# Moving the loads of v, one token-order turn and the start's memsets in a fused attention and MLP kernel

## The chip, the cores and the metric

The kernel runs on one core of a Trainium2 chip. The metric is the device time of one execution in microseconds (us), the median of several runs. A profiled execution gives the trace; its span (317.2 us for the kernel before) is a little shorter than the timed figure.

The core's engines run their own instruction streams in order and meet at semaphores: PE (TensorE, matmuls), DVE (VectorE), ACT (ScalarE), POOL (GpSimd) and SP (SyncE, which here only issues transfers). POOL issues transfers too.

## The reference: what is computed

Attention over 8 batch rows with 8 heads, 576 tokens and 64 channels a head, and then an MLP with a squared relu over all 4608 tokens:

```python
scores = scale * np.matmul(q, k.transpose(0, 1, 3, 2))
rel = pos[:, None] - pos[None, :]
mask_plain = (rel >= 0) & (rel < 32)                        # heads 0 to 3: sliding
mask_dil = (rel >= 0) & (rel < 128) & (rel % 4 == 0)        # heads 4 to 7: dilated
attn = softmax(where(mask, scores, -1e9))
x = (attn @ v).transpose(0, 2, 1, 3).reshape(4608, 512)
g = np.maximum(x @ w_in, 0) ** 2                            # w_in: 512 x 2048
out = g @ w_out                                             # w_out: 2048 x 512
```

"Row" below is a batch row (0 to 7), "block" is a group of 512 tokens of the MLP (0 to 8). The MLP of block b - 1 is computed while the attention of row b is.

## The kernel before

q and k of rows 0 and 1 are transposed on the PE. For row 2 onward they go another way. POOL loads q and k of the sliding heads into `ns` and copies those of the dilated heads to DRAM as fp16 (`dd`). A copy engine writes `ns` in token order into `nr`. SP stores `nr` to DRAM (`dp`) and then reads `dp` and `dd` back with transposing transfers into `QKTp` and `QKTd`:

```python
    def by_token(b, n):
        r = natp.tile([P, 9, HH, D], FP16, name=f"nr{b}", tag="n")
        (nc.gpsimd if b == 2 else nc.vector).tensor_copy(
            r.rearrange("x j h d -> x h j d"), n.rearrange("x h (j d) -> x h j d", d=D)
        )
        return r
    # keep_sliding_qk: two nc.sync.dma_start, dp <- nr
    # transpose_sliding: two nc.sync.dma_start_transpose, QKTp <- dp
    # transpose_dilated: two nc.sync.dma_start_transpose, QKTd <- dd
```

v is loaded by SP in fp32 into the single buffers `sv` (sliding heads) and `sd` (dilated heads), and POOL casts them to fp16 into `vp` and `vd`, of which there are two each:

```python
    def load_v(b):
        load_sliding_v(b)              # two transfers into sv
        load_dilated_v(b, nc.sync)     # two transfers into sd

    def cast_v(b):
        cast_sliding_v(b)              # three POOL copies, vp[b % 2] <- sv
        cast_dilated_v(b)              # four POOL copies, vd[b % 2] <- sd
```

Before POOL loads q and k of a further row it reads one element of the last transpose of the current one:

```python
    def after_transposes(b):
        t = QKTp[b % 2][...] if b == 2 else QKTd[b % 2][...]
        nc.gpsimd.tensor_copy(seen, t)
```

The main loop over the rows. `pump(n)` puts n pieces of the pending MLP work into the instruction streams; `hooks` are called inside the attention of the row: 2 and 3 behind the two groups of dilated scores, 4 to 6 behind the three sliding products with v:

```python
    for b in range(2, B):
        pending.append(moe_gen(b - 1))
        nxt = b + 1
        hooks = {}
        if nxt < B:
            after_transposes(b)
            ns = load_sliding_qk(nxt)
            if b == 2:
                cast_v(b)
            dd = keep_dilated_qk(nxt)
            if b > 2:
                load_v(nxt)
                cast_v(nxt)

            def turn():
                dp = keep_sliding_qk(nxt, by_token(nxt, ns))
                transpose_sliding(nxt, dp)
                transpose_dilated(nxt, dd)
                if b == 2:
                    load_v(nxt)
                    cast_v(nxt)

            hooks[{3: 6}.get(b, 3)] = turn
        first, gap, gap2 = {2: (24, 4, 2), 3: (16, 3, 3)}.get(b, (8, 3, 3))
        pump(first)
        attn_scores(b, gap, 0, hooks)
        attn_values(b, gap2, False, hooks)
        pump(1000)
```

The start: q and k of row 0 are loaded, the masks of the two head groups are built on DVE from an iota on POOL, buffers are cleared, and only then does DVE come to the first copy behind the PE's transposes:

```python
    nsd = {0: load_qk(0)}
    nc.vector.memset(sv[0:PADP, :, 0, :], 0.0)
    nc.vector.memset(sd[0:64, 0, :, :], 0.0)
    nc.gpsimd.iota(reli, ...)
    # ... warm-up of the ScalarE table
    nc.vector.tensor_copy(relf, reli)
    # ... nine DVE instructions: lo_, hi_, maskp / maskd
    nc.vector.memset(sv[0:PADP, :, 1:NB, :], 0.0)
    nc.vector.memset(AT[:, :, UW:640], 0.0)
    for r in range(2):
        # ... five small memsets of QKTp, QKTd, vp, vp, vd, and one compare into vd
    # ...
    nc.vector.tensor_copy(sv[64:P, 0, :, 0], n[0:64, 0, 0:NB])
    load_sliding_v(0)
    nc.vector.tensor_copy(sd[64:P, :, 0, 0], n[0:64, 0, 0:2])
    load_dilated_v(0, nc.sync)
    cast_sliding_v(0, (0, 2))
    load_w_in()
```

The row's MLP work, as far as it matters here: `ph` (PE) is x times w_in, `rt` (ACT) its relu, `g` (DVE) the square; `gs` are sums of `g` on DVE for a Strassen form of the second product, whose results `pa`, `pb`, `pc` are taken by ACT and DVE into `ou` and `ov` and stored.

Of the kernel before, what the change touches and what calls it, by code (L numbers as in the profile page):

```python
# [9 lines left out]
FP32 = mybir.dt.float32  # L10
I16 = mybir.dt.int16
ALU = mybir.AluOpType
ACTF = mybir.ActivationFunctionType
P = 128
# [3 lines left out]
def kernel(  # L18
# [9 lines left out]
    nc = tc.nc  # L28

    B, H, S, D = q.shape  # L30
# [16 lines left out]
    NB = S // QB  # L47
    PADP = P - QB
# [4 lines left out]
    KPAD = 64  # L53
    UW = 576

    const = ctx.enter_context(tc.tile_pool(name="const", bufs=1))
# [29 lines left out]
    QKTp = [const.tile([P, 2, 2, PADP + S], FP16, name=f"QKTp{r}") for r in range(2)]  # L86
    QKTd = [const.tile([P, 2, 2, KPAD + S], FP16, name=f"QKTd{r}") for r in range(2)]
    AT = const.tile([P, 8, 640], FP16, name="AT")
    vp = [const.tile([P, NB, HH, D + 2], FP16, name=f"vp{r}") for r in range(2)]
    vd = [const.tile([P, 2, DIL, HH, D + 2], FP16, name=f"vd{r}") for r in range(2)]  # L90
    sv = stg.tile([P, HH, NB, D], FP32, name="sv")
# [6 lines left out]
    def load_qk(b):  # L98
        n = load_sliding_qk(b)
        m = natp.tile([P, 36 * D], FP16, name=f"nd{b}", tag="n")  # L100
        for i, s in ((1, k), (0, q)):
            nc.gpsimd.dma_start(
                out=m[64 * i : 64 * (i + 1), :],
                in_=s[b, HH:H].rearrange("h (p j) d -> (h p) (j d)", j=36),
            )
        return n, m

    def load_sliding_qk(b):
        n = natp.tile([P, HH, 9 * D], FP16, name=f"ns{b}", tag="n")
        for i, s in ((1, k), (0, q)):  # L110
            nc.gpsimd.dma_start(
                out=n[64 * i : 64 * (i + 1)],
                in_=s[b, 0:HH].rearrange("h (p j) d -> p h (j d)", j=9),
            )
        return n
# [8 lines that stand above are left out]
    def load_sliding_v(b):  # L124
        vv = v[b, 0:HH].rearrange("h (m p) d -> p h m d", p=QB)
        if b == 0:
            for m in range(NB):
                nc.sync.dma_start(out=sv[PADP:P, :, m, :], in_=vv[:, :, m, :])
        else:
            for h in (0, 2):  # L130
                nc.sync.dma_start(out=sv[PADP:P, h : h + 2], in_=vv[:, h : h + 2])

    def load_dilated_v(b, eng):
        vv = v[b, HH:H].rearrange("h (i c) d -> i h (c d)", c=DIL)
        i0 = 0
        for t in range(2):
            eng.dma_start(out=sd[P - OWND[t] : P, t, :, :], in_=vv[i0 : i0 + OWND[t]])
            i0 += OWND[t]

    def load_v(b):  # L140
        load_sliding_v(b)
        load_dilated_v(b, nc.sync)
# [25 lines left out]
    def cast_sliding_v(b, ms=range(0, NB, 2)):  # L168
        for m in ms:
            nc.gpsimd.tensor_copy(  # L170
                vp[b % 2][:, m : m + 2, :, 0:D], sv[:, :, m : m + 2, :].rearrange("p h m d -> p m h d")
            )

    def cast_dilated_v(b):
        for t in range(2):
            p0 = 64 * t
            for c in range(0, DIL, 2):
                nc.gpsimd.tensor_copy(  # L178
                    vd[b % 2][p0:P, t, c : c + 2, :, 0:D],
                    sd[p0:P, t, :, D * c : D * (c + 2)].rearrange("p h (c d) -> p c h d", d=D),  # L180
                )
# [12 lines left out]
    def cast_v(b):  # L194
        cast_sliding_v(b)
        cast_dilated_v(b)


    def keep_dilated_qk(b):
        d = dpool.tile([2, HH * CL, DIL * D], FP16, name=f"dd{b}", tag="dd")  # L200
        for i, src in ((1, k), (0, q)):
            nc.gpsimd.dma_start(
                out=d[i].rearrange("(r i) x -> r (i x)", i=4),
                in_=src[b, HH:H].rearrange("h (r i) d -> (h r) (i d)", i=16),
                max_dma_last_dim=4096,
            )
        return d

    def keep_sliding_qk(b, r):
        d = dpool.tile([2, S, HH * D], FP16, name=f"dp{b}", tag="dp")  # L210
        for i in (1, 0):
            nc.sync.dma_start(
                out=d[i].rearrange("(p j) x -> p (j x)", j=9),
                in_=r[64 * i : 64 * (i + 1)].rearrange("p j h d -> p (j h d)"),
            )
        return d

    def transpose_sliding(b, dp):
        for i in (1, 0):
            nc.sync.dma_start_transpose(out=QKTp[b % 2][:, i, :, PADP:], in_=dp[i])  # L220

    def transpose_dilated(b, dd):
        for i in (1, 0):
            nc.sync.dma_start_transpose(out=QKTd[b % 2][:, i, :, KPAD:], in_=dd[i])
# [4 lines left out]
    def after_transposes(b):  # L229
        t = QKTp[b % 2][:, 0, 1, PADP : PADP + 1] if b == 2 else QKTd[b % 2][:, 0, 1, KPAD : KPAD + 1]  # L230
        nc.gpsimd.tensor_copy(seen, t)


    nsd = {0: load_qk(0)}
    nc.vector.memset(sv[0:PADP, :, 0, :], 0.0)
    nc.vector.memset(sd[0:64, 0, :, :], 0.0)
    reli = const.tile([P, QB], I16, name="reli")
    nc.gpsimd.iota(reli, pattern=[[1, QB]], base=0, channel_multiplier=-1)
    make_identity(nc, ident)
    warm = const.tile([P, 1], FP32, name="warm")  # L240
    nc.vector.memset(warm, 0.0)
    nc.scalar.activation(warm, warm, ACTF.Exp)

    relf = const.tile([P, QB], FP32, name="relf")
    nc.vector.tensor_copy(relf, reli)
# [3 lines left out]
    for m, w, pad in (  # L249
# [12 lines left out]
            lo_[:, 0:w].unsqueeze(1).to_broadcast([P, m.shape[1], w]),  # L262
            hi_[:, 0:w].unsqueeze(1).to_broadcast([P, m.shape[1], w]),
        )
    nc.vector.memset(sv[0:PADP, :, 1:NB, :], 0.0)
    nc.vector.memset(AT[:, :, UW:640], 0.0)
    for r in range(2):
        nc.vector.memset(QKTp[r][:, 1, :, 0:PADP], 0.0)
        nc.vector.memset(QKTd[r][:, 1, :, 0:KPAD], 0.0)
        nc.vector.memset(vp[r][:, :, :, D : D + 1], 1.0)  # L270
        nc.vector.memset(vp[r][0:PADP, 0, :, D : D + 1], 0.0)
        nc.vector.memset(vd[r][:, 1, :, :, D : D + 1], 1.0)
        nc.vector.tensor_scalar(
            out=vd[r][:, 0, :, :, D],
            in0=relf[:, 0:1].unsqueeze(2).to_broadcast([P, DIL, HH]),
            scalar1=-PADD[0] + 0.5,
            scalar2=None,
            op0=ALU.is_lt,
        )
# [3 lines left out]
    for t, w in zip(wi, wi_cols):  # L283
        r = t.rearrange("p d (g f s) -> p d g f s", f=P, s=4)
# [196 lines left out]
    def moe_gen(c):  # L481
        g = hidden(c)
        yield from mm1_gen(c, g, c > 1)
        yield from (mm2_strassen_gen if c > 1 else mm2_gen)(c, g)
# [10 lines left out]
    def pump(n):  # L495
        for _ in range(n):
            while pending:
                try:
                    next(pending[0])
                    break  # L500
                except StopIteration:
                    pending.pop(0)
# [159 lines left out]
    def attn_scores(b, gap, less=0, hooks={}):  # L662
        for hp in range(2):
            s_sliding(b, hp)
            if hp in hooks:
                hooks[hp]()
            pump(gap)
        for g in range(2):
            s_dilated(b, g)
            if 2 + g in hooks:  # L670
                hooks[2 + g]()
            if g:
                halo_sliding(b, 0)
            pump(gap - less)
# [110 lines left out]
# [7 lines that stand above are left out]
            if b == 2:  # L792
                cast_v(b)
            dd = keep_dilated_qk(nxt)
            if b > 2:
                load_v(nxt)
                cast_v(nxt)

            def turn():
                dp = keep_sliding_qk(nxt, by_token(nxt, ns))  # L800
                transpose_sliding(nxt, dp)
                transpose_dilated(nxt, dd)
                if b == 2:
                    load_v(nxt)
                    cast_v(nxt)

            hooks[{3: 6}.get(b, 3)] = turn
        first, gap, gap2 = {2: (24, 4, 2), 3: (16, 3, 3)}.get(b, (8, 3, 3))
        pump(first)
        attn_scores(b, gap, 0, hooks)  # L810
        attn_values(b, gap2, False, hooks)
        pump(1000)
# [33 lines left out]
```

The softmax here doesn't subtract the row's maximum and nothing guards it: scores larger than these inputs give would overflow.

## Time and profile before

| what | figure |
|---|---|
| median of 3 runs | 319.86 us (319.48 to 320.25) |
| span of the profiled execution | 317.2 us |
| PE busy | 293.3 us, 92% |
| DVE busy | 215.6 us, 68% |
| ACT busy | 184.0 us, 58% |
| POOL busy | 73.2 us, 23% |
| moved by transfers | 43.58 MB, mean 137 GB/s |

Busy time is the time in which an engine has an instruction under way. It is an average over quite different stretches of the kernel, so the slices and the tables by stretch are read along with it. A line such as "DVE nr L119 <- DMA ns<-in_q_dram: 1.9, 1, 1.9" says that DVE, at the instruction of line 119 that writes nr, waited 1.9 us in total, once, at most 1.9 us, and that what ended last was the transfer of q into ns. In a timeline line the first two numbers are the start and the duration in us, and the bracket holds the idle time ahead and what ended it.

### The profile page before, as it was taken

The numbers are of one execution on the slowest core, as the hardware profiler recorded it, in microseconds if no ns is written. First come the engines' busy times: TensorE is split into PE (matmuls) and PEld (weight loads), VectorE is DVE, ScalarE is ACT, GpSimd is POOL, SyncE is SP. The second block draws the span as 40 slices with busy tenths as digits, with TensorE's granted clock in tenths as the row PEclk, the third lists the DMA queues.
The fourth block names the chain that finished last, engine by engine and source line by source line (L and its number), as shares of the span: only waits on it lengthen the run. The fifth ranks groups of instructions, "written<-read, shape, count | busy, mean of one in ns | idle before, by whom it ended". The sixth has DMA issues, their size and how long they took to land.

```text
span 317.2 us, 7107 instructions
## 1 busy us (share of the span) xinstructions
PE 293.3 (92%) x2874; PEld 195.7 (62%) x2874; DVE 215.6 (68%) x433; ACT 184.0 (58%) x326; POOL 73.2 (23%) x114
## 2 busy tenths in 40 slices
PE   1688998999999989998899999989999999999994
PEld 1344554554455468655698978448855885685583
DVE  5875447668942999469937994699468944744652
ACT  2665648668646972596239933885289426615620
POOL 4381026414600870124240702060000000000000
PEclk9999999999999999999999999999999999999999
DMA  7699998899789994999779689957030012003003
GB/s 120 156 209 214 206 162 141 169 206 216 110 164 212 267 177 99 248 192 216 149 118 274 134 133 151 252 108 149 18 118 0 2 46 88 0 3 133 2 0 132
DMA packets 67024, 43.58 MB, mean 137 GB/s; under 512 B 48624, under 2 KB 59376, under 8 KB 66992
## 3 DMA queue, kind: packets, MB, share of 16 engines
q1 hardware_dynamic: 57920, 28.45, 41.4%
q0 software_dynamic: 9072, 14.68, 26.9%
q8 instruction: 22, 0.36, 0.5%
q14 instruction: 10, 0.08, 0.1%
HBM read 36.70 MB, written 16.52 MB: 168 GB/s over the span
## 4 chain that ended last, share of the span: by engine, by line
PE 57%; DVE 21%; DMA 10%; ACT 6%; issue 2%; SPq 2%; POOL 1%; DVEq 0%; POOLq 0%
PE ph L293 20%; PE pa L370 12%; PE pb L370 8%; PE po L436 6%; DVE g L317 5%; DMA ns<-in_q_dram 5%; DVE AT L547 3%; ACT AT L546 3%; PE pc L370 3%; DMA sv<-in_v_dram 3%; DVE x_p L590 3%; PE paw L618 2%; DMA QKTp<-dp 2%; ACT rt L316 2%; DVE gs L327 2%
## 5 line engine op out<-in xcount | busy, mean ns | idle before, releaser
L293 PE MATMUL ph<-xT,wi 128*128 128x512 f16 (+1 forms) x640 | 133.4, 359 | 0.7 <-ACT xT L657 0.7
L316 ACT ACTIVATE rt<-ph 128x512 f16<-128x512 f32 x144 | 85.1, 603 | 36.9 <-PE ph L293 34.7
L293 PEld LDWEIGHTS <-wi 128*128 128x128 f16 x640 | 68.6, 114 | 46.8 <-issue 0.8
L317 DVE TENSOR_TENSOR g<-rt 128x512 f16<-128x512 f16 x144 | 66.2, 467 | 42.8 <-ACT rt L316 41.8
L370 PEld LDWEIGHTS <-g 128*128 128x128 f16 x448 | 42.2, 98 | 7.2 <-DVE g L401 0.9
L170 POOL CAST vp<-sv 128x512 f16<-128x512 f32 x24 | 17.5, 759 | 85.5 <-DMA sv<-in_v_dram 26.6
L370 PEld LDWEIGHTS <-gs 128*128 128x128 f16 x336 | 31.5, 98 | 6.0 <-DVE gs L327 2.6
L436 PE MATMUL po<-wo,g 128*128 128x512 f16 x128 | 33.1, 379 | 0.0
L370 PE MATMUL pa<-wt,gs 128*128 128x256 f16 x224 | 28.9, 273 | 1.8 <-DVE gs L327 1.7
L397 DVE TENSOR_TENSOR ov<-pb,ov 128x512 f32<-128x512 f32 x14 | 9.7, 691 | 29.5 <-PE pb L370 18.2
L370 PE MATMUL pb<-wt,g 128*128 128x256 f16 x224 | 27.7, 273 | 0.4 <-DVE g L401 0.4
L178 POOL CAST vd<-sd 128x512 f16<-128x512 f32 (+1 forms) x32 | 24.9, 805 | 2.6 <-DMA sd<-in_v_dram 1.1
L386 ACT COPY ov<-pa 128x512 f32<-128x512 f32 x14 | 8.2, 585 | 29.7 <-PE pa L370 29.7
L590 DVE TENSOR_TENSOR x_d<-paw,rcp_d 72x512 f16<-72x512 f32 x32 | 22.0, 686 | 1.1
L546 ACT ACTIVATE AT<-pz 128x576 f16<-128x576 f32 x32 | 20.0, 712 | 2.2 <-PE pz L575 2.0
L546 ACT ACTIVATE AT<-ps 128x576 f16<-128x576 f32 x32 | 19.2, 662 | 3.3 <-PE ps L556 3.1
L547 DVE TENSOR_TENSOR AT<-AT,maskp 128x576 f16<-128x576 f16 x32 | 17.4, 560 | 4.5 <-ACT AT L546 2.7
L657 ACT COPY xT<-py 128x576 f16<-128x576 f16 x16 | 10.2, 640 | 15.6 <-PE py L651 15.4
L547 DVE TENSOR_TENSOR AT<-AT,maskd 128x576 f16<-128x576 f16 x32 | 16.7, 541 | 2.8 <-ACT AT L546 1.1
L590 DVE TENSOR_TENSOR x_p<-pav,rcp_p 96x512 f16<-96x512 f32 x24 | 16.5, 687 | 0.8
L386 ACT COPY ou<-pa 128x512 f32<-128x512 f32 x14 | 8.2, 588 | 14.6 <-PE pa L370 14.6
L604 PEld LDWEIGHTS <-AT 128*128 128x128 f16 x192 | 9.1, 97 | 11.5 <-issue 7.8
(81 smaller groups left out, 311.9 us busy)
## 6 DMA issues: line engine op xcount, KB each, us to landing
sv<-in_v_dram SPq DMA_DIRECT2D x14, 288.0 KB, 6.8
dp<-nr SPq DMA_DIRECT2D x12, 288.0 KB, 3.7
out_dram<-ou SPq DMA_DIRECT2D x6, 512.0 KB, 3.3
out_dram<-ov SPq DMA_DIRECT2D x6, 512.0 KB, 3.6
sd<-in_v_dram SPq DMA_DIRECT2D x8, 320.0 KB, 8.1
ns<-in_k_dram POOLq DMA_DIRECT2D x8, 288.0 KB, 5.8
ns<-in_q_dram POOLq DMA_DIRECT2D x8, 288.0 KB, 6.6
sd<-in_v_dram SPq DMA_DIRECT2D x8, 256.0 KB, 6.7
```

Source lines behind the costliest of these rows:

```text
L170: nc.gpsimd.tensor_copy(vp[b % 2][:, m : m + 2, :, 0:D], sv[:, :, m : m + 2, :].rearrange("p h m d -> p m h d"))
L178: nc.gpsimd.tensor_copy(vd[b % 2][p0:P, t, c : c + 2, :, 0:D], sd[p0:P, t, :, D * c : D * (c + 2)].rearrange("p h (c d) -> p c h d", d=D),)
L293: nc.tensor.matmul(ph[:, t0:t1], wi4[ffc // 4][:, dmk, :, ffc % 4], xT[:, dmk, x0 : x0 + t1 - t0], start=(dmk == 0 and t0 == 0), stop=(dmk ...
L316: nc.scalar.activation(rt, ph[:], ACTF.Relu)
L317: nc.vector.tensor_mul(g[:, ffc, :], rt, rt)
L370: nc.tensor.matmul(banks[bank][:, t], a(k, t), b(k), start=(new and t == 0 and k == 0), stop=(k == HF - 1), skip_group_check=True,)
L386: nc.scalar.copy(ot, banks[A])
L436: nc.tensor.matmul(po, g[:, ffc, t * P : (t + 1) * P], wo[ffc // 4][:, ffc % 4, :], start=(ffc == 0), stop=(ffc == NFF - 1),)
L546: nc.scalar.activation(AT[:, u, 0:UW], ps[:, :, 0 : UW // 2], ACTF.Exp, scale=scale)
L547: nc.vector.tensor_mul(AT[:, u, 0:UW], AT[:, u, 0:UW], mask)
L590: nc.vector.tensor_tensor(out=x[0:w], in0=pv[:, :, :, 0:D], in1=rcp[0:w].unsqueeze(3).to_broadcast([w, 2, HH, D]), op=ALU.mult,)
L657: nc.scalar.copy(xT[:, 2:4, t0 : t0 + 288].rearrange("x c (i r) -> x c i r", r=DIL), py[:, 0:UW].rearrange("x (c r i) -> x c i r", c=2, r= ...
```

## The change

It has three parts.

- The memsets of the start, and the warm-up of ScalarE's table, come ahead of the mask work in DVE's stream, where they depend on nothing.
- v of the next row is loaded by SP behind the store of `dp` and ahead of the transposes, for every row from 3 on. Before, from row 4 on it was loaded at the beginning of the loop's turn, together with q and k; for row 3 it was loaded behind the transposes. The casts of v follow it in the source; POOL's own stream keeps its order.
- Row 4 is turned (copied in token order, stored and transposed) behind row 3's scores as the other rows are, and not behind the last sliding product with v.

The aim is to keep v's transfers apart from those of q and k, to have v ready for the casts while SP waits for `dp` anyway, and to let DVE use the time in which it waits for the iota.

```diff
@@ start
     nsd = {0: load_qk(0)}
+    warm = const.tile([P, 1], FP32, name="warm")
+    nc.vector.memset(warm, 0.0)
+    nc.scalar.activation(warm, warm, ACTF.Exp)
     nc.vector.memset(sv[0:PADP, :, 0, :], 0.0)
     nc.vector.memset(sd[0:64, 0, :, :], 0.0)
+    nc.vector.memset(sv[0:PADP, :, 1:NB, :], 0.0)
+    for r in range(2):
+        nc.vector.memset(QKTp[r][:, 1, :, 0:PADP], 0.0)
+        nc.vector.memset(QKTd[r][:, 1, :, 0:KPAD], 0.0)
+        nc.vector.memset(vp[r][:, :, :, D : D + 1], 1.0)
+        nc.vector.memset(vp[r][0:PADP, 0, :, D : D + 1], 0.0)
+        nc.vector.memset(vd[r][:, 1, :, :, D : D + 1], 1.0)
+    nc.vector.memset(AT[:, :, UW:640], 0.0)
     # ... iota, identity, masks; the same memsets are taken out below them
@@ loop
             if b == 2:
                 cast_v(b)
             dd = keep_dilated_qk(nxt)
-            if b > 2:
-                load_v(nxt)
-                cast_v(nxt)
 
             def turn():
                 dp = keep_sliding_qk(nxt, by_token(nxt, ns))
+                load_v(nxt)
                 transpose_sliding(nxt, dp)
                 transpose_dilated(nxt, dd)
-                if b == 2:
-                    load_v(nxt)
-                    cast_v(nxt)
-
-            hooks[{3: 6}.get(b, 3)] = turn
+                cast_v(nxt)
+
+            hooks[3] = turn
```

More of the change, by code (lines that the diff above doesn't have):

```diff
@@ L239 @@
     make_identity(nc, ident)
-    warm = const.tile([P, 1], FP32, name="warm")
-    nc.vector.memset(warm, 0.0)
-    nc.scalar.activation(warm, warm, ACTF.Exp)
     relf = const.tile([P, QB], FP32, name="relf")
@@ L264 @@
         )
-    nc.vector.memset(sv[0:PADP, :, 1:NB, :], 0.0)
-    nc.vector.memset(AT[:, :, UW:640], 0.0)
     for r in range(2):
[L268 to L272, printed above, removed]
         nc.vector.tensor_scalar(
```

## The prediction

> **What bounds the kernel now.** I read the page's slices first, then the PE waits, the timeline of the first 14 us, the busy table by row, and last the queue timelines of SP and POOL.
>
> ```profile
> PE   1688998999999989998899999989999999999994
> DMA  7699998899789994999779689957030012003003
> PE pt L519 <- DMA ns<-in_k_dram: 5.2, 1, 5.2
> PE ps L556 <- DVE QKTp L166: 2.4, 1, 2.4
> ```
>
> A slice is 7.9 us. The PE is full nearly everywhere but in the first slices, so a gain has to come from the start or from holes of a few tenths of a slice. The list of PE waits says the same: 5.2 us for the first load, 2.4 us for a DVE copy, and nothing else above 1.7 us. So I ask why that copy is late (timeline of the first 14 us, DVE):
>
> ```profile
> 2.15 0.06 DVE L241 MEMSET warm<- 128x1 f32 x1
> 4.10 0.21 DVE L245 CAST relf<-reli 128x96 f32<-128x96 int16 x1 [1.90 <-POOL reli L238]
> 6.31 0.31 DVE L260 TENSOR_TENSOR maskd<-lo__137,hi__138 128x288 f16<-128x288 f16 x1
> 6.82 1.12 DVE L265 MEMSET sv<- 32x1280 f32 x1 [0.20 <-issue]
> 9.43 1.42 DVE L166 COPY QKTp<-pt 128x576 f16<-128x576 f16 x2
> ```
>
> DVE stands idle for 1.90 us waiting for POOL's iota, then builds the masks, and only then does memsets that depended on nothing; the copy that the PE awaits sits behind them.
>
> Second, one row against another. A row's stage runs from one block's first ph matmul to the next block's (from the chain in order of time). The busy tables of those stretches (columns: stretch, length, busy us and count of PE, PEld, DVE, ACT, POOL; clock, DMA share, GB/s), rows 3 to 7:
>
> ```profile
> 97.12:130.14 33.02, 31.55 (x318) 21.72 (x316) 25.89 (x47) 21.00 (x38) 13.32 (x19) 1.00 0.98 189
> 130.14:164.80 34.66, 31.89 (x316) 21.32 (x315) 25.42 (x48) 20.16 (x37) 11.32 (x17) 1.00 0.90 182
> 164.80:197.29 32.49, 32.08 (x383) 28.45 (x382) 24.79 (x48) 20.23 (x37) 8.46 (x12) 1.00 0.91 173
> 197.29:229.81 32.52, 31.23 (x318) 21.67 (x316) 25.23 (x48) 20.16 (x37) 5.48 (x7) 1.00 0.62 133
> 229.81:261.00 31.19, 31.04 (x317) 21.87 (x316) 22.82 (x47) 19.99 (x37) 0.00 (x0) 1.00 0.10 36
> ```
>
> All five do the same matmuls. Row 7 prepares no further row: no POOL work, no token-order copy (nr), almost no DMA; with PE busy 31.04 of 31.19 it is the **floor**. Rows 3 to 6 are longer by 1.83, 3.47, 1.30 and 1.33 us; that 7.9 us is all that the row part of the change can win. Row 4 stands out. Its wait is in the list of waits, its cause in the SP timeline:
>
> ```profile
> DVE nr L119 <- DMA ns<-in_q_dram: 1.9, 1, 1.9
> 121.72 1.17 SPq L212 DMA_DIRECT2D dp<-nr  x2
> 128.11 3.10 SPq L224 DMA_TRANSPOSE QKTd<-dd  x2
> 132.82 2.18 SPq L131 DMA_DIRECT2D sv<-in_v_dram  x2
> 143.75 1.14 SPq L212 DMA_DIRECT2D dp<-nr  x2
> ```
>
> Row 4 was turned late (dp at 121.7). Its dilated transposes were therefore issued only at 128.1, POOL (which reads QKTd into "seen" before it may load the next q and k) went on at 133.6, q and k of row 5 were issued at 134.2 and 134.8, and landed 6.9 and 8.1 us later among the loads of v and the stores, so nr of row 5 held DVE from 141.0 to 142.97.
>
> **What the Trainium skill says.** Perfetto Trace Analysis, "Tensor Engine Instruction (MATMUL, LD_WEIGHTS)": ACT, DVE and GpSimd are strict FIFO, and the PE's end times are modelled. The trace agrees on the first: no DVE work runs in the 1.9 us that nr waits. "DMA: Bandwidth & Descriptors", "Issuing engines are not separate DMA queues": transfers of all issuers interleave on the same 16 engines. It agrees too: between 132 and 150 us one half of sd took 14.0 us to land while ns, dd and an out store ran, against 6.7 us between 84 and 104. "SBUF — State Buffer", "Who interferes with whom": DVE and GpSimd share one port pair under an exclusive lock. The trace shows the effect, not a total block: g<-rt takes 422 ns on average in row 7, where POOL is idle, and 539 in row 3, with up to 865 single.
>
> **The change, part by part.** No operation is added or removed. The PE, ACT and POOL run the same sequence as before; on DVE the memsets and one nr move, on SP the v loads.
>
> *Memsets first.* Moved ahead of the mask work: sv 1.12 us, AT 0.27, ten small ones together about 0.7 (8.22 to 9.09 holds them and two short compares), 2.1 in all. They fill the 1.90 us idle, so relf starts at about 4.35 instead of 4.10. The masks take 2.52 as now (4.10 to 6.62), so they end at 6.9; the two compares and the two copies into sv and sd take about 0.5; the QKTp copy can start at 7.45 instead of 9.43. Is its input there? ACT copies its own half of the same transposes at 7.38, so yes, just. The scores then start at about 8.3 instead of 10.24: 1.9 us earlier. The first v load waits for the same DVE queue (SP waits 8.7 us for "sd L708"), so it moves too, into a hole: the DMA digits of the first 16 us are at 3 or below between about 8.8 and 10.4 us. w_in is issued behind POOL's first casts of v, so it follows. I count **1.7**, a little less than 1.9, because DMA is near full from 16 to 40 us and may give some of it back.
>
> *Row 4 turned behind row 3's scores.* nr of row 4 moves from 120.9 to about 112.9 less what has been won, 8 us earlier. So the transposes of row 4, its "seen", and row 5's q and k come some 6 us earlier, even with v in front of the transposes; the DVE wait of 1.9 us ends. *v behind dp.* It takes v out of the time when q, k and out stores move (131 to 147 us) and puts it where dp is being written and SP otherwise waits for it (16.5 us in five waits). It also moves POOL's casts, 5.5 us a row. Now rows 3 and 4 are both cast in row 3's stage (103.2 to 108.6 and 112.9 to 119.1), in the middle of the chain of DVE work that leads to the PE. Then row 3's come at about 93 to 98, where DVE has gaps, and those of rows 4 to 7 some 9 to 15 us behind nr; the dense DVE stretch ends about 12.6 us behind nr (row 5: 175.84 to 188.4), so half of each is out of it.
>
> What that is worth: DVE's excess over row 7 is 3.07, 2.60, 1.97 and 2.41 us in rows 3 to 6. Against the excess length, 1.83, 1.54 (3.47 less the wait of 1.93), 1.30 and 1.33, about 0.6 us of length comes with 1 us of DVE. After the change 0.75 (nr) and half of a contention of 1.2 (row 5: 1.97 less 0.75) remain, 1.35 us, which is 0.8 of length. Row 3 could win 1.0, row 4 2.7, rows 5 and 6 0.5 each. I take 0.9, 2.5, 0.4 and 0.4: **4.2**. Sum with the start: 5.9.
>
> **The rivals.** (a) *A new wait at nr of row 4.* It is 8 us earlier, so its q and k must be as well. They follow "seen" of row 3, which now stands at 108.7 behind POOL's casts. With v behind dp, the casts are done at about 98, but QKTd is pushed back by v: issued 93.4 to 97.3 now, about 2 us later then, landing (4.2 us) near 103; q and k issued at 103 land at 110 to 111. nr is due at 112.85 less some 3 us won by then. That is a tie: I give 0.4 to a stall of about 1.5 us, and take 0.6 off. (b) *DMA swallows the start.* If wi or row 1's loads are bound by bandwidth from 16 to 41 us (DMA share 1.1 to 1.2 there), the 1.7 shrinks; against it, no PE wait for a DMA occurs there now, and the hole that is filled lies ahead of it. The result would be about 316. (c) *The PE is the bound and DVE's relief is worth nothing*: then rows 3, 5 and 6 give nothing, only the start and the wait: about 316.2. (d) *Transposes behind v come too late.* Row 5's sliding scores come 25 us after nr, QKTp would land at about 13; only if v took over 10 us more would PE wait. Then 319 or more; unlikely.
>
> **Range and chances.** 319.86 less 5.9 plus 0.6 gives 314.6. All steps in full, without a stall, give about 312.5; the start or the rows alone, with a stall, give 316 to 317. Over 2% faster means below 313.46: 0.27. Slower than 326: 0.02.
>
> **What would show it.** QKTp copy at about 7.5 and first ps near 8.3; no DVE idle for reli (right for the start). No wait "nr <- ns" in row 4, whose stage is then about 32.2 long; row 3 about 32.1, rows 5 and 6 about 32.1; casts of row 3 before 100. Wrong if nr of row 4 waits over 2 us for ns, if PE waits for QKTp or QKTd behind v, if ph of block 0 starts later than 26 (27.48 now), or if the casts lengthen g<-rt as much as now.

## The result and the profile after

The changed kernel takes **309.68 us** (median of 4 runs, 308.76 to 310.76), against 319.8 us for the kernel before on the same chip: a ratio of 0.9684 with an interval of 0.9646 to 0.9722. The span of the profiled execution falls from 317.2 to 307.3 us. The prediction said 314.6 us, at best about 312.5: the direction was right, and the size was about half of what came.

The page of the kernel after, its slices of PE:

```profile
PE   1798998999999999999999999999999999999994
```

Before, the PE row had eights in four slices of rows 3 to 6; now it is nines from the eighth slice to the last but one.

The start, from the timeline of the first 14 us, DVE lines and then one line of PE (start and duration in us):

```profile
4.38 0.27 DVE L247 MEMSET AT<- 128x256 uint32 x1
4.58 0.13 DVE L253 CAST relf<-reli 128x96 f32<-128x96 int16 x1
7.42 1.42 DVE L166 COPY QKTp<-pt 128x576 f16<-128x576 f16 x2
8.23 0.66 PE L557 MATMUL ps<-QKTp 64*128 64x96 f16 x12 [0.40 <-DVE QKTp L166]
```

The memsets run until relf begins, and relf carries no bracket: DVE no longer idles for the iota. The copy of QKTp begins at 7.42 instead of 9.43, the scores at 8.23.

The busy tables of rows 3 to 7 of the kernel after, with the columns of the table shown for the kernel before (stretch, length, busy us and count of PE, PEld, DVE, ACT, POOL; clock, DMA share, GB/s):

```profile
94.55:126.29 31.74, 31.37 (x317) 21.78 (x316) 23.66 (x47) 21.00 (x38) 10.20 (x18) 1.00 1.10 197
126.29:157.48 31.19, 31.04 (x318) 21.94 (x317) 23.32 (x48) 19.99 (x37) 9.42 (x16) 1.00 0.98 176
157.48:188.75 31.27, 31.16 (x381) 28.60 (x380) 23.33 (x48) 20.00 (x37) 9.82 (x14) 1.00 0.88 168
188.75:219.94 31.19, 31.04 (x318) 21.88 (x316) 23.32 (x48) 19.99 (x37) 6.58 (x8) 1.00 0.85 169
219.94:251.13 31.19, 31.04 (x317) 21.90 (x316) 22.82 (x47) 19.99 (x37) 0.00 (x0) 1.00 0.10 35
```

Read the second column first: rows 4, 5 and 6 are as long as row 7, which prepares nothing. POOL still works 6.6 to 9.8 us in each of them, and DVE has only 0.50 us more than in row 7, for one instruction more, the copy nr (0.75 us by itself). So in these rows both the wait and the rest of DVE's excess are gone, and nr that remains costs no length. Row 3 stays 0.55 us above the floor; g still takes 482 ns on average there. The rows give 1.28, 3.47, 1.22 and 1.33 us, and what lies ahead of row 3 gives 2.57 (97.12 less 94.55). The sum, 9.87, is the fall of the span.

What DVE lost, in the groups of row 5 (count, busy us and mean ns of one, idle ahead). First the kernel before:

```profile
L317 DVE TENSOR_TENSOR g<-rt 128x512 f16<-128x512 f16 x16 | 7.6, 491 | 2.3 <-ACT rt L316 2.2
L326 DVE TENSOR_TENSOR gs<-g 128x1024 f16<-128x1024 f16 x2 | 1.7, 839 | 0.1
```

The same groups after:

```profile
L318 DVE TENSOR_TENSOR g<-rt 128x512 f16<-128x512 f16 x16 | 6.7, 422 | 2.4 <-ACT rt L317 2.2
L327 DVE TENSOR_TENSOR gs<-g 128x1024 f16<-128x1024 f16 x2 | 1.4, 692 | 0.1
```

A g takes 422 ns, as in row 7, where POOL is idle. The timelines of POOL say why. First its two stretches of casts for row 6 in the kernel before:

```profile
175.99 2.56 POOL L170 CAST vp<-sv 128x512 f16<-128x512 f32 x3 [13.93 <-ACT vp L185]
178.82 3.42 POOL L178 CAST vd<-sd 128x512 f16<-128x512 f32 x4 [0.28 <-DMA sd<-in_v_dram]
```

The same after:

```profile
177.70 3.33 POOL L170 CAST vp<-sv 128x512 f16<-128x512 f32 x3 [19.49 <-ACT ou L387]
180.99 3.38 POOL L178 CAST vd<-sd 128x512 f16<-128x512 f32 x4
```

Each has to be held against DVE's nr and the last of the row's four gs of 1024 columns (a later one of 2048 columns, on the subtraction's result, is not counted here). Before, nr began at 175.82 and the last gs ended at 186.41: all seven casts fall into the run of g and gs. After, nr begins at 168.32 and the last gs ends at 177.48, and the casts begin at 177.70, just behind it. In rows 4 and 6 they begin 1.8 and 0.3 us behind it.

### The profile page after: what moved, and what is told of

Read it like the earlier page. It is cut to its first block, busy times and chain, and to the rows that moved or that the text cites. A ratio compares the mean times of both kernels' runs of the same rounds, so it can differ in the third digit from the quotient of the medians.

```text
span 307.3 us, 7108 instructions
## 1 busy us (share of the span) xinstructions
PE 290.7 (95%) x2874; PEld 196.5 (64%) x2874; DVE 207.9 (68%) x433; ACT 183.4 (60%) x326; POOL 71.7 (23%) x114
## 4 chain that ended last, share of the span: by engine, by line
PE 71%; ACT 10%; DVE 7%; DMA 6%; issue 2%; SPq 2%; POOL 1%; POOLq 0%; DVEq 0%
PE ph L294 27%; PE pa L371 16%; PE pb L371 8%; PE po L437 7%; ACT AT L547 5%; DMA ns<-in_q_dram 5%; PE pc L371 4%; ACT rt L317 3%; PE paw L619 3%; PE pav L605 2%; PE px L634 1%; PE py L652 1%; DVE AT L548 1%; DMA QKTp<-dp 1%; PE pf L491 1%
## 5 line engine op out<-in xcount | busy, mean ns | idle before, releaser
L318 DVE TENSOR_TENSOR g<-rt 128x512 f16<-128x512 f16 x144 | 62.2, 435 | 42.7 <-ACT rt L317 41.1
L371 PEld LDWEIGHTS <-gs 128*128 128x128 f16 x336 | 31.6, 98 | 3.7 <-DVE gs L328 0.3
L178 POOL CAST vd<-sd 128x512 f16<-128x512 f32 (+1 forms) x32 | 24.2, 782 | 3.1 <-DMA sd<-in_v_dram 2.4
L548 DVE TENSOR_TENSOR AT<-AT,maskd 128x576 f16<-128x576 f16 x32 | 14.9, 484 | 2.6 <-ACT AT L547 0.6
L640 ACT COPY xT<-px 128x576 f16<-128x576 f16 x16 | 10.2, 638 | 9.2 <-PE px L634 8.6
```

What stands on the lines that cost most here:

```text
L178: nc.gpsimd.tensor_copy(vd[b % 2][p0:P, t, c : c + 2, :, 0:D], sd[p0:P, t, :, D * c : D * (c + 2)].rearrange("p h (c d) -> p c h d", d=D),)
L318: nc.vector.tensor_mul(g[:, ffc, :], rt, rt)
L371: nc.tensor.matmul(banks[bank][:, t], a(k, t), b(k), start=(new and t == 0 and k == 0), stop=(k == HF - 1), skip_group_check=True,)
L548: nc.vector.tensor_mul(AT[:, u, 0:UW], AT[:, u, 0:UW], mask)
L640: nc.scalar.copy(xT[:, 0:2, t0 : t0 + 288], px[:, 0:UW].rearrange("x (c t) -> x c t", c=2),)
```

## The experiments

Three theories were set against one another for rows 3 to 6. **C**: POOL's casts of v lengthen the DVE operations on which the PE waits (g, gs, mask products); moved away from them, all of that length comes back. **D**: v's transfers delay the transfers of q and k, and so nr. **P**, the prediction's own reading: the length of a row goes with its DVE excess at 0.6 us for 1 us, whatever that excess is, so nr costs length too.

Row stages below run from one mark to the next. The mark is the second addition of pb into ov, which can be found in every run; row 3, which has none ahead of it, begins with its first ph in the PE timeline. By these marks the kernel before has its first ph at 27.48, row 3 at 96.96, and rows 3 to 7 of 33.2, 34.8, 32.3, 32.5 and 31.2 us; the kernel after has 25.06, 94.38 and 32.0, 31.2, 31.3, 31.2, 31.2. A median stands beside the ratio to the kernel before on the same chip. In the traces of two of these kernels (the start alone, and nr made twice) the granted clock falls to 0.50 for 3 to 4 us between 24 and 30 us, and the 60 ph matmuls that begin there take 14.8 us instead of 13.1; it is named where it matters.

### The two halves

The memsets alone, and the row loop alone (both are the matching part of the diff of the change).

> Only the start of the change: the memsets and the warm-up come first, the row loop is that of before. The start is one cause, the rows another, and they add. First matmul of block 0 at 25.1 as after (27.5 before), rows 3 to 6 as long as before (33.0, 34.7, 32.5, 32.5). Time 319.8 less 2.4 = 317.4. If the rows need the earlier start to win (for instance because a load is then ready in time), row 4 would get shorter too and the time fall below 316.5.

> Only the row loop of the change, the start as before. If start and rows add: first matmul of block 0 at 27.5, row 3 near 31.7, rows 4 to 6 near 31.2, time 319.8 less 7.3 = 312.5. If the earlier start is needed, rows 3 and 4 stay above 32.5 and the time above 314.

Measured: the start alone 317.88 us (0.9964, 0.9939 to 0.999), the loop alone **312.26** (0.9777, 0.9709 to 0.9845). With the start alone the first ph comes at 24.92, as early as in the full change, but row 3 begins at 96.15: in its profile the clock is at 0.61 from 24 to 28 us, so 0.8 us of the 2.5 stays. The stages of rows 3 to 7 are 33.3, 34.1, 32.3, 32.9, 31.2, near those of before; row 4 is 0.7 us shorter, because its nr waits 1.3 us for q and not 1.9. With the loop alone they are 31.9, 31.2, 31.3, 31.2, 31.2, those of after. But for that wait the two parts do not touch each other's stages. Because a difference of 2 us rests on it, both were repeated on one chip with the full change, five rounds each:

> The kernel after, unchanged, beside the two halves of the change on one chip. Ratio to before 0.968 as measured first, about 309.9 where before is 320.

> Only the row loop of the change, once more, beside after on one chip. If the start carries its 2.4 us (first matmul of block 0) through to the end, this is 2.4 longer than after, ratio 0.976; if row 2's wait for its transposes (QKTp) swallows part of it, it is only about 1.2 longer, ratio 0.972.

> Only the start of the change, once more, on the same chip. Carried through: ratio 0.9925 (317.6 of 320). Half swallowed by row 2's wait, by row 4's wait or by the clock: 0.996, as it was measured first.

Measured: full change 309.70 (0.9707, 0.9671 to 0.9742), loop alone 312.45 (0.9797, 0.9757 to 0.9836), start alone 318.21 (0.9955, 0.9931 to 0.9979). So the start is worth 1.4 us by itself (0.45% of 319.8) and 2.75 us (312.45 less 309.70) on top of the loop's part. The intervals allow 0.7 to 2.2 us for the one and, by the two ratios, about 1.2 to 4.6 for the other; they overlap, so that the start is worth more there is not shown. The single traces do not settle it either. In the two loop-alone traces row 2's scores wait 2.2 and 1.6 us for their transposes (QKTp), in the full change 0.5 and 0.9. But these transposes are issued ahead of the loop, where the loop-alone kernels run the program of before, and the six other traces with the same start have waits of at most 0.8 us there: this is a spread of executions, not an effect of the loop. In the repeat of the start alone the PE waits 2.8 us for the q of row 0 (1.1 before), so that its first ph comes only at 26.00, and 0.9 us more in row 2.

### The loop's two parts, one at a time

v behind dp, with row 4 still turned late:

```diff
-            hooks[3] = turn
+            hooks[{3: 6}.get(b, 3)] = turn
```

> Before, with v of the next row loaded behind the store of dp and cast later, in all rows from 3 on; row 4 is still turned behind the last sliding product with v. Theory C (the casts on POOL lengthen the DVE operations g and gs while the PE waits for them): rows 5 and 6 fall from 32.5 to 31.2 each, row 3 to about 32, while row 4 keeps or lengthens its wait for q and k of row 5 (2 to 4 us, since v now stands in front of row 4's transposes). Time about 316.5 to 318. Theory D (the collision of v's transfers with q and k is what costs): the wait in row 4 goes too although row 4 is turned late, row 4 below 33, time below 315.5.

And the early turn alone, in the kernel before:

```diff
-            hooks[{3: 6}.get(b, 3)] = turn
+            hooks[3] = turn
```

> Before, with row 4 turned behind row 3's scores as all others, v still loaded at the loop's beginning. Row 4's q and k are issued at 109.3 there, behind row 3's casts on POOL, and land about 116 to 117; the copy nr stands in DVE's stream at 112.9, so DVE waits about 4 us in row 3. Row 4's wait of 1.9 us for row 5 goes. Theory C and D both: rows 5 and 6 stay at 32.5, time 319 to 322: this part alone wins nothing. If the turn by itself were what won in row 4, the time would be 317.5 to 318.

Measured: v behind dp alone 314.66 (0.9851, 0.9781 to 0.9922), rows 31.4, 34.1, 31.3, 31.2, 31.2; the early turn alone **323.24**, slower by an interval that only just leaves out 1 (1.0101, 1.0002 to 1.0201), rows 40.1, 32.3, 32.4, 32.7. The first takes rows 3, 5 and 6 to the floor or within 0.2 us of it, which C foretold, and more out of row 3 than expected. It moves transfers and casts together, so it does not yet tell C from D in these rows. Row 4 keeps its wait, as the list of DVE waits of that run shows:

```profile
DVE nr L119 <- DMA ns<-in_q_dram: 2.0, 1, 2.0
```

The second shows why the early turn needs the first: row 4's q and k are not there yet. The timeline of the early turn alone (DVE, then the busy table of two stretches of 4 us; the last three columns are clock, DMA share, GB/s):

```profile
119.65 0.76 DVE L119 COPY nr<-ns 128x2304 f16<-128x2304 f16 x1 [5.42 <-issue]
116.00:120.00 4.00, 0.00 (x0) 0.00 (x0) 0.35 (x1) 0.00 (x0) 2.34 (x4) 0.93 1.16 206
120.00:124.00 4.00, 1.94 (x16) 1.53 (x17) 3.90 (x10) 1.21 (x2) 0.00 (x0) 0.50 0.81 194
```

DVE stands 5.42 us in front of nr, the PE then waits 6.6 us for x_p, and comes back at half its clock. Row 3 grew by 7 us where 4 were expected; the wait is longer than expected, and the clock adds to it. The cause of the wait is on POOL: the casts of row 3's v run from 104.97 to 110.36, "seen" stands behind them, q of row 4 is issued at 111.67 and lands 7.9 us later. In the kernel after those casts are done at 98.9, and q of row 4 goes out at 102.95. On top of v behind dp the same line of code wins 2.4 us (314.66 less 312.26), and row 4 falls from 34.1 to 31.2. The run also shows what the early turn does to row 4 when nothing else changes: its wait is gone and the stage is 32.3 instead of 34.8, with the casts still among its g (495 ns on average).

### Casts or transfers

The casts of v held back on POOL until the next row's transposes have landed; the transfers stay as in the kernel before:

```diff
             if b > 2:
                 load_v(nxt)
-                cast_v(nxt)
 ...
                 transpose_dilated(nxt, dd)
                 if b == 2:
                     load_v(nxt)
-                    cast_v(nxt)
+                else:
+                    nc.gpsimd.tensor_copy(seen, QKTp[nxt % 2][:, 0, 1, PADP : PADP + 1])
+                cast_v(nxt)
```

> Before, with v of rows 4 to 7 loaded as early as before, but POOL made to wait for QKTp of the next row ahead of its casts, so that only the casts move (to about 10 us behind nr), not the transfers; row 4 is still turned late. Theory C (casts lengthen g and gs on DVE while the PE waits for them): rows 5 and 6 fall from 32.5 to 31.3 each, g<-rt there from about 490 to 425 ns; row 3 loses row 4's casts and falls to about 32.2; time about 316 to 317. Theory D (v's transfers collide with those of q and k): nothing of the transfers has changed, rows 5 and 6 stay at 32.4 and the time at 319.

Measured: 316.74 (0.9864, 0.9835 to 0.9894), rows 31.7, 35.4, 31.3, 31.2, 31.2. With v's transfers left where they were, rows 5 and 6 fall to the floor and row 3 to 31.7. Row 5 of this run (busy table, then its group of g):

```profile
165.31:196.59 31.28, 31.17 (x381) 28.56 (x380) 23.33 (x48) 20.01 (x37) 8.19 (x13) 1.00 0.83 161
L317 DVE TENSOR_TENSOR g<-rt 128x512 f16<-128x512 f16 x16 | 6.7, 422 | 2.4 <-ACT rt L316 2.2
```

Length, DVE and g are those of the kernel after. D is out for these rows. Row 4 still waits, and behind the wait its clock is at half for 3 us:

```profile
DVE nr L119 <- DMA ns<-in_q_dram: 3.2, 1, 3.2
```

Next, the casts left out altogether for rows 4 to 7, which therefore compute with the v of rows 2 and 3, and then the loads of v left out for these rows with the casts kept, which therefore cast an old v again:

```diff
             if b > 2:
                 load_v(nxt)
-                cast_v(nxt)        # first kernel
```

```diff
             if b > 2:
-                load_v(nxt)        # second kernel
                 cast_v(nxt)
```

> Before, with the casts of v of rows 4 to 7 left out (vp and vd keep old rows; all transfers stay). Theory C: rows 5 and 6 at 31.2 to 31.3, as in the kernel after, although nr with its 0.75 us stays in DVE's stream: nr alone costs no length. My reading in the prediction (0.6 us of length for each us of DVE, nr included): rows 5 and 6 at 31.65. Theory D: 32.4. Row 4 keeps its wait of about 1.9 us: about 33. Time near 315.5 by C.

> Before, with the loads of v of rows 4 to 7 left out and the casts kept (they cast what lies in sv and sd). They then start when POOL has issued q and k, earlier than before, among the scores. Theory D: rows 5 and 6 at 31.3, time 315.5. Theory C: the casts still meet g, gs and the mask products, rows 5 and 6 at 32 or more. Both: q and k of row 5 land faster without v, so row 4's wait of 1.9 us shrinks to under 1. Time by C about 317.5 to 318.5.

Measured: without the casts 312.75 (0.983, 0.9755 to 0.9904), rows 32.1, 33.0, 31.3, 31.2, 31.2; without the loads 317.18 (0.9907, 0.9877 to 0.9937), rows 38.0, 31.6, 31.3, 31.2, 31.2. The busy table of row 6 without casts:

```profile
193.04:224.23 31.19, 31.04 (x317) 21.89 (x316) 23.33 (x48) 20.00 (x37) 0.00 (x0) 1.00 0.63 139
```

POOL does nothing, nr is still there (DVE 23.33 against 22.82 in row 7), and the row is at the floor: nr costs no length in it. Row 4's wait for q stays, at 2.4 us, and yet the stage falls from 34.8 to 33.0: its casts had cost length too.

The second kernel is a miss for C's number: rows 5 and 6 were to stay at 32 or above and came to 31.3 and 31.2. Without a load to wait for, the casts moved as well, so the run changed two things. One line of its POOL timeline shows where to:

```profile
162.93 1.74 POOL L170 CAST vp<-sv 128x512 f16<-128x512 f32 x3
```

The three take 1.74 us, not 2.56: they fall near the beginning of the row's ph, where DVE has gaps, and lengthen little. Rows 5 and 6 of this run thus do not separate C from D. In row 3 the casts of the next row begin 3 us behind those of the row itself and run without a pause. One gs on DVE is held for most of the time that they last:

```profile
110.82 3.60 DVE L327 TENSOR_TENSOR gs<-gs,g 128x1024 f16<-128x1024 f16 x1
111.03 1.74 POOL L170 CAST vp<-sv 128x512 f16<-128x512 f32 x3
```

It takes 3.60 us where 0.69 is usual, while the three casts, and four more that end at 115.68, nearly keep their pace; the PE then waits 3.7 us for x_p. This is the collision at its largest; with a clock at half behind that wait, row 3 comes out 5 us longer.

Row 4's wait is gone in this run, but it does not prove D either: row 3 had become longer, so that row 5's q was issued 2.1 us into row 4 instead of 4.7. **Row 4's wait** is a race between the issue of q, its landing and nr, and the runs together tell its terms. Before, q was issued at 134.84 and took 8.1 us. With v behind dp alone it took 5.7 us, but was issued at 137.08, since v now stood ahead of the transposes and the wait stayed at 2.0. In the kernel after it is issued at 129.47, takes 6.3 us, and is there 1.3 us ahead of nr (137.1). So only the early turn's earlier issue ends the wait. The landing is shorter in both kernels with v moved, as D would have it, but with no v at all (the run just shown) it still took 7.2 us, so that v is what lengthens it is not shown.

### The costs put back by themselves

Into the kernel after, behind nr of rows 4 to 6, seven idle casts of the size of v's, on tiles of their own (they add work and change no output):

```diff
+                if b > 3:
+                    nc.gpsimd.tensor_copy(gate, nr[:, 8, 3, D - 1 : D])
+                    for _ in range(7):
+                        nc.gpsimd.tensor_copy(ddst, dsrc)
                 load_v(nxt)
```

> After, with seven idle casts (128x512, fp32 to fp16, on tiles of their own) put on POOL right behind nr in rows 4, 5 and 6, about where the casts of v of rows 6 and 7 stood before; they wait for nothing but nr and nothing waits for them. No transfer is added or moved. Theory C: g and gs there lengthen and rows 4 to 6 grow from 31.2 to 32.0 to 32.5 each, time 309.7 plus 3 = about 312.7. Theory D: nothing changes, 309.7.

And instead of them, nr made twice, which adds 0.75 us of DVE a row and nothing on POOL:

```diff
                 nr = by_token(nxt, ns)
+                nc.vector.tensor_copy(nr..., ns...)    # the same copy again
                 dp = keep_sliding_qk(nxt, nr)
```

> After, with the token-order copy nr made twice in the rows where DVE makes it (rows 2 to 6), 0.75 us of DVE more in each and nothing else. By the prediction's reading (0.6 us of length for each us of DVE): 0.45 more in each, 2.2 in all, about 312. If DVE has that much room ahead of the PE in these rows and only the collision with the casts used it up: rows 4 to 6 stay within 0.2 of 31.2, time 309.7 to 310.3.

Measured: with idle casts 313.67 (0.9792, 0.9753 to 0.9831), rows 32.2, **32.4, 32.2, 32.4**, 31.2; with nr twice 313.17 (0.9772, 0.9731 to 0.9813), rows 32.7, **31.3, 31.4, 31.3**, 31.2. The groups of row 5 with the idle casts:

```profile
L322 DVE TENSOR_TENSOR g<-rt 128x512 f16<-128x512 f16 x16 | 7.5, 482 | 2.3 <-ACT rt L321 2.2
L331 DVE TENSOR_TENSOR gs<-g 128x1024 f16<-128x1024 f16 x2 | 1.7, 838 | 0.1
```

These are the figures of the kernel before (491 and 839) within 2%. The busy tables of row 6, first with the idle casts and then with nr twice:

```profile
192.03:224.45 32.42, 31.65 (x317) 21.63 (x316) 24.94 (x49) 20.11 (x37) 12.89 (x15) 1.00 0.79 155
```

```profile
192.91:224.23 31.32, 31.17 (x317) 21.69 (x316) 23.80 (x49) 20.09 (x37) 7.84 (x10) 1.00 0.92 167
```

Against row 6 of the kernel after (31.19, DVE 23.32), the idle casts put 1.62 us on DVE and 1.23 on the length; the second nr puts 0.48 on DVE and 0.13 on the length. C is shown directly, and P is out for rows 4 to 6. The time of the second kernel is nearly as long as that of the first all the same. Its profiled span is 4.3 us longer than that of the kernel after, and only 0.3 of that is in rows 4 to 6. The slower clock behind 25 us takes 1.7. Most of the rest are two waits of the PE behind the second nr, which the kernel after has not (the first) or has at 0.2 us (the second):

```profile
PE pav L605 <- DVE rcp_p L590: 0.9, 1, 0.9
PE pav L605 <- DVE x_p L591: 1.0, 1, 1.0
```

The second is in row 3, which is 0.8 us longer. DVE comes to nr 15.49 us behind the row's first ph in both kernels, and to x_p 0.79 us later than in the kernel after: 0.75 us of DVE costs all of its length there. The first is in row 2, where about half of the delay stands ahead of nr already. So a further copy is free only where DVE has room ahead of the PE, as in rows 4 to 6. Why row 3 has none was not followed up. The two medians alone would have misled: the stages carry the verdict.

### Tries to go further

The copy of row 0's halo moved behind the copies of QKTd, and that with one filling product less at the start:

```diff
-    halo_sliding(0, 0)
     # ... t_dilated(0, m, a, False) for all m, a
+    halo_sliding(0, 0)
```

> After, with the first halo copy of row 0 on ACT moved behind the copies of the dilated transposes, since in the kernel after ACT waits 0.61 us for POOL's cast of v there and holds the copies of QKTd. If that wait is on the path, the first matmul of block 0 comes at 24.6 instead of 25.1 and the time is 309.2; if v's landing is, nothing moves.

> After, with the first halo copy moved as in the run before and only one filling matmul in place of two each time in row 0 (the fills compute nothing that is used; they keep the PE busy while row 0's attention has no other work for it). If the fills are on the path, block 0 starts 0.5 to 1.5 us earlier, time about 308.7. If the PE needs them for its clock, the granted clock falls below full in the first slices and block 0's matmuls take longer: 310 or more.

Measured: 309.5 (0.9728, 0.9662 to 0.9793) and 310.3 (0.9693, 0.9658 to 0.9728): nothing won. The first has its first ph at 25.54 and not at 24.6. The second has it at 24.30, 0.8 us earlier, but row 3 begins at 95.79, later than in the kernel after; the list of PE waits tells where it went:

```profile
PE ps L557 <- DMA QKTp<-dp: 2.3, 1, 2.3
```

Row 2's transposes into QKTp were issued at 67.86, against 65.62 in the kernel after, chiefly because those into QKTd held SP's queue for 7.4 us instead of 5.8; so the scores waited. No version tried here beats the change.

## Why the prediction was wrong

**The start: mechanism right, size low.** The three marks came as worked out: relf at 4.58 (said 4.35), QKTp's copy at 7.42 (7.45), first scores at 8.23 (8.3). The term was 1.7; the trace has 2.42 at the first ph and 2.57 at row 3, the medians 1.4 alone and 2.75 with the loop's part. The discount for a DMA that gives some back was not needed. About 0.3 us more came from a place the working did not look at: in timelines of row 0's dilated scores, three mask products take 2.09 us instead of 2.38, because they now meet fewer of POOL's casts of vd.

**Row 4's wait: right, and the discount wrong.** The wait is gone and the stage fell by 3.47, where 2.5 was taken. Rival (a) did not happen: "seen" of row 3 was read at 101.7 (said 103), q and k of row 4 were issued at 102.95 at the latest and landed near 109.5, and nr came at 109.87 without a wait. The tie was won by 0.4 us. The repeat of the kernel after has no wait there either, so the 0.6 us taken off was not needed. The early turn alone lost that race by 5.4 us, so the worry had its ground.

**The failed step is the price of DVE's excess.** The prediction divided excess length by excess DVE time, got 0.6 us of length per us, and applied it to nr and collision alike, with half of the collision left over. For rows 4 to 6 both halves of that are refuted. First, nr: a row with nr and no casts is at the floor, and a second nr adds 0.1 us. (In row 3 the second nr added 0.8: a price there is, but by the row, not one for all.) Second, the remainder: none of the collision is left. It was larger than the 1.2 us taken, too, since DVE lost 1.46 us in row 5 (24.79 less 23.33). The prediction put the casts 9 to 15 us behind nr, and they came 9 to 16 behind it (177.70 less 168.32 in row 5). It also had a dense stretch of DVE that lasts until 12.6 us behind nr. But the operations in that stretch are not alike. Those that the casts lengthened, g and gs, end 9.2 us behind the start of nr (177.48 less 168.32). What follows was not lengthened in the kernel after: x_d reads from PSUM, and the large subtraction behind it kept its 1.21 us while the casts stretched (in row 3 of the kernel before it took 1.63 beside casts, so this was not certain). The right sum for rows 4 to 6 is this: the collision at about 0.75 us of length per us (1.23 over 1.62 with the idle casts), and nr at zero. That gives back 1.2 to 1.3 us in rows 5 and 6 where 0.4 was taken, 1.28 in row 3 where 0.9 was, and most of the missing 1.0 in row 4.

The terms together: said 1.7, 0.9, 2.5, 0.4, 0.4 and minus 0.6; found 2.57, 1.28, 3.47, 1.22 and 1.33. The three excesses of rows 4 to 6 make 2.7 of the 4.6 us missed, the start 0.9, the discount 0.6, row 3 0.4. The prediction's upper end, "all steps in full", kept the wrong price, and that is why the range missed. Its own terms in full (1.9, 1.0, 2.7, 0.5 and 0.5) give 313.3 and not 312.5.

**Rivals (b), (c), (d).** DMA did not swallow the start in the full change. Rival (c) held for nr in rows 4 to 6, whose relief is worth nothing, but not for the casts. Rival (d) did not come either. From the SP timeline of the kernel after in row 3:

```profile
110.65 1.16 SPq L212 DMA_DIRECT2D dp<-nr  x2
111.90 2.24 SPq L131 DMA_DIRECT2D sv<-in_v_dram  x2
114.23 2.01 SPq L137 DMA_DIRECT2D sd<-in_v_dram  x2
116.34 5.70 SPq L220 DMA_TRANSPOSE QKTp<-dp  x2
```

v fills 4.3 us of the queue behind dp's store, and the transposes follow without a gap at 116.34; QKTp landed 8.2 us after that at the latest, and no PE wait for a transpose in rows 4 to 7 is in the list.

**What is settled and what not.** Shown: casts beside g, gs and the mask products are the length in rows 5 and 6 (moved, left out and put back) and part of it in row 3 (moved and left out); row 4's wait ends with the early turn, and the early turn wins only together with v's move. Row 4's other part is its casts: without them, the wait left in place, it falls by 1.9 us, with the early turn and the casts in place it stays 1.1 above the floor, and idle casts put 1.2 back. Open: how much of row 3's fall is row 4's casts and how much its own; why a second nr costs length in row 3 and not in rows 4 to 6; and whether the start is worth more beside the loop's part than alone.

## What to carry to other kernels

Ahead of pricing an engine's excess time, ask which of its operations the bound engine waits for and which of those a neighbour lengthens: 5.5 us of POOL casts cost 1.2 to 1.3 us a row among g and gs, and nothing from 0.2 us behind the last of them. Fit a price from several rows only if the rows differ in one thing; here every row with casts had nr as well, and one row without casts but with nr would have shown that nr was free in rows 4 to 6. Move a transfer and the work that waits for it together with the step that needs the room: the same line that won 2.4 us behind the moved v lost about 3 us without it (0.1 to 6 by the interval).

## What was not expected of the hardware

**Which DVE operations the casts lengthen.** The Trainium skill, "SBUF — State Buffer", section "Who interferes with whom", says that a DVE instruction with two SBUF inputs contends with a GpSimd instruction that reads SBUF, that one with at most one SBUF input outside the 2-port modes does not, and that issue order decides who blocks. The runs agree on which operations suffer: g (both inputs in SBUF) went from 422 to 482 ns on average beside idle casts and gs from 692 to 838, while x_d, which reads its product from PSUM, stayed at 687 throughout. In the kernel after it is the casts that stretch, to about 1.1 us each (3.33 us for three), beside an SBUF subtraction of DVE that keeps its 1.21 us. Two things go beyond this. nr, a copy with one input, took 1.16 us instead of 0.75 beside casts in row 6 of the kernel before, so one input alone does not make an operation safe; whether the exception for 2-port modes covers this copy, no run here shows. And the gs of 3.60 us was held over several casts in a row, although by the trace it began 0.2 us ahead of the first; the prediction's "not a total block" was read from milder cases, and the order of the starts in the trace does not tell which side is held. The prediction had the effect and did not sort the operations by where their inputs lie; that sorting would have brought the failed step nearer to the truth.

**What a wait of the PE costs beyond its length.** The Trainium skill, "TensorE: Matmul & The Clock Gate", section "The HAM clock gate", has the clock fall to half after a window of about 3.4 us idle and rise again after one busy. The early turn alone agrees: idle for 6.6 us, then a clock of 0.50 from 120 to 124 us and 0.72 in the next 4, full again at 128. So does the run without loads of v: 3.7 us idle, then 0.50 from 117 to 123. But with the casts held back the PE was idle for only 2.43 us (to 146.31), and the clock was at 0.50 from 147 to 150: the length that the page gives is no safe limit, and the measurement decides. Even gaps may be enough: in the start alone and with nr twice the PE was busy for about 60% of the 3 to 4 us before the clock fell near 25 us, without a long wait; the kernel after, with much the same gaps there, kept its full clock in both of its traces. What such a fall costs can be read behind 25 us: 60 ph matmuls take 14.8 us instead of 13.1. A wait of the PE of 2.4 us or more can thus cost 1.7 us beyond its length. Rows without such a wait ran at 1.00.
